# A spectral filter beside a gated MLP on one core: a stored order of instructions, four-tile butterflies, and final sums copied by ScalarE

## The chip, the cores and the metric

The kernel runs on one NeuronCore of a Trainium2 chip. The core has five engines with a queue of their own each: TensorE (PE, matmul), VectorE (DVE), ScalarE (ACT), GpSimd (POOL) and SyncE (SP), which here issues the DMAs. An engine takes its instructions in the order in which they stand in its queue, and waits on semaphores for what others produce. The metric is device time in microseconds of one execution; lower is better.

## The reference

For x of 2048 rows and 640 columns (bf16) two branches are computed on the normalised rows and added to x:

```python
xn = _layernorm(x, axis=-1)
return x + _A_ref(xn, A_w_r, A_w_i) + _B_ref(xn, B_w_gate, B_w_up, B_w_down)
# A: X = rfft2(xn) * (w_r + 1j*w_i); irfft2(X) to bf16
# B: g = xn @ w_gate; u = xn @ w_up; (g * u) @ w_down      640 -> 1536 -> 640
```

A is a two-dimensional Fourier transform over rows and columns, a product with a spectrum of weights, and the way back. B is a gated MLP without an activation function.

## The kernel before

The 2048 rows lie in 16 row tiles of 128 partitions. Everything is held on chip; only inputs, tables and outputs cross to HBM.

Start. The rows are loaded (`_X_LOADS`), normalised by tile (L767 and L776 on ScalarE, or L785 and L794 on VectorE, for the statistics; L807, L811, L817 for the inverse deviation; L824 subtracts, L831 scales), and transposed: the first four tiles on TensorE (L849), the other twelve by DMA (L837). While nothing is ready, TensorE runs 40 matmuls on zeros (L749) and, behind the first transpose, 44 small filler matmuls (L738). The gate and up projections of the first four tiles use 128 or 256 columns at a time (L998), the rest 512 columns (L978). Their results are copied from PSUM by a helper (L718 where ScalarE does it, L719 where VectorE does) and multiplied on VectorE (L1014, L1015).

Row transform. A column transform of 640 points is split into butterflies on VectorE and matmuls. The forward butterflies work on two row tiles at a time: five tasks S1 to S5, 14 instructions (L891 to L925), eight groups. R (L938) is the matmul that follows, for each row tile.

Middle. Only when all 16 tiles have passed R may D begin (L1056), then C (L1079), the product with the spectrum of weights WM on VectorE (L1094, L1097), a negation NG (L1106, L1107) and reversed copies NS on GpSimd (L1114 to L1116), then IA, the inverse (L1130, L1131). This runs over 16 steps t of two q each. The spectrum is loaded in a ring of three buffers.

End. I (L1159) for each row tile, then the inverse butterflies V1 to V5, two row tiles at a time (L1183 to L1216, 13 instructions, eight groups), whose last result is the branch's bf16 value. For each row tile and half of its columns, ACC (L1237) sums twelve down-projection matmuls in one PSUM bank, and IV (L1249) adds the spectral branch with one more matmul. FIN (L1257) adds x from PSUM on VectorE, half by half, and SP stores each half.

What sets the order. The kernel is written as tasks with engine choices, durations, priorities and reads and writes. `plan` (L155) is a list scheduler that runs while the kernel is built: it picks one task after another by priority and earliest start, chooses the engine and the PSUM bank (with a cap on banks per class, such as two for L998's and three for the middle's tasks), and drops fillers that no longer fit. `compute_waits` (L339) then puts in the semaphore waits. What is built is a fixed order on each engine; L1272 calls the scheduler. The order decides all below.

```python
sch.caps = {"glu": opts.get("cap_glu", 4), "acc": opts.get("cap_acc", 5), "fill": 1}
...
sch.plan(8, filler_deadline=opts.get("fill_deadline", 7600.0))
sch.compute_waits()
```

Of the kernel before, what the change touches and what calls it, by code (L numbers as in the profile page):

```python
# [17 lines left out]
_DMA_ISSUE = 500.0  # L18


class _Task(object):
    __slots__ = ("tid", "name", "engs", "dur", "emit", "prio", "deps", "nleft", "succ", "bank", "frees",
                 "freers", "eng", "start", "end", "seq", "units", "nbytes", "semkey", "semval", "cls", "vc",
                 "waits")
# [47 lines left out]
class _Sched(object):  # L72
    def __init__(self):
        self.tasks = []
        self.bufs = []
        self.caps = {}
        self.window = 250.0
        self.affinity = 600.0
        self.dma_bw = _DMA_BW
        self.slack = {"pe": 1000.0, "act": 300.0, "dve": 400.0, "pool": 100.0, "sp": 0.0}  # L80
        self.order = None
        self.urgent = ()
        self.makespan = 0.0
# [71 lines left out]
    def plan(self, nbanks=8, filler_deadline=0.0):  # L155
        tasks = self.tasks
        for t in tasks:
            t.succ = []
        for t in tasks:
            t.deps.discard(t)  # L160
            for d in t.deps:
                d.succ.append(t)
            t.nleft = len(t.deps)
        eng_free = dict((e, _START) for e in _ENGS)
        seq = dict((e, 0) for e in _ENGS)
        banks = [[0.0, None] for _ in range(nbanks)]
        held_by_cls = {}
        avail = [t for t in tasks if t.nleft == 0]
        pending_free = {}
        for t in tasks:  # L170
            if t.bank is not None:
                if not t.freers:
                    raise RuntimeError("task %s takes banks but nothing frees them" % t.name)
                pending_free[t.tid] = len(t.freers)
        free_end = {}
        dma_pipe = 0.0
        order = dict((e, []) for e in _ENGS)
        nsch = 0
        ntot = len(tasks)
        dropped = []  # L180

        def choose(kind):
            best = None
            if kind == "pair":
                for k in range(0, nbanks, 2):
                    a_, b_ = banks[k], banks[k + 1]
                    if a_[0] is None or b_[0] is None:
                        continue
                    ft_ = max(a_[0], b_[0])
                    if best is None or ft_ < best[0]:  # L190
                        best = (ft_, k)
            else:
                for k in range(nbanks):
                    st = banks[k]
                    if st[0] is None:
                        continue
                    partner = banks[k ^ 1]
                    pen = 0.0 if partner[0] is None else 1.0
                    key = (pen, st[0])
                    if best is None or key < best[2]:  # L200
                        best = (st[0], k, key)
            return best

        def release(p):
            k0 = p.units[1]
            nb = 2 if p.units[0] == "pair" else 1
            for k in range(k0, k0 + nb):
                banks[k][0] = free_end[p.tid]
                banks[k][1] = list(p.freers)
            held_by_cls[p.cls] -= 1  # L210

        while nsch < ntot:
            cands = []
            for t in avail:
                unit_choice = None
                bank_ready = 0.0
                if t.bank is not None:
                    cap = self.caps.get(t.cls)
                    if cap is not None and held_by_cls.get(t.cls, 0) >= cap:
                        continue  # L220
                    ch = choose(t.bank)
                    if ch is None:
                        continue
                    unit_choice = (t.bank, ch[1])
                    bank_ready = ch[0]
                    if bank_ready > 0.0:
                        bank_ready += _XLAT["pe"]
                best = None
                for ei, e in enumerate(t.engs):
                    est = eng_free[e]  # L230
                    for d in t.deps:
                        lat = _SLAT[e] if d.eng == e and not d.nbytes else _XLAT[e]
                        if d.eng == e and e == "pe":
                            lat = -_TAIL[e]
                        de = d.end + lat
                        if de > est:
                            est = de
                    if bank_ready > est:
                        est = bank_ready
                    fin = est + t.dur[e]  # L240
                    score = fin + (self.affinity if ei > 0 else 0.0)
                    if best is None or score < best[3]:
                        best = (est, fin, e, score)
                cands.append((best[0], best[1], best[2], t, unit_choice))
            real = [c for c in cands if c[3].cls != "fill"]
            if not cands or (not real and nsch + len([a_ for a_ in avail if a_.cls == "fill"]) < ntot
                             and not any(c[3].cls == "fill" for c in cands)):
                raise RuntimeError("scheduler deadlock: %d/%d scheduled, avail=%s" % (
                    nsch, ntot, [a_.name for a_ in avail][:10]))
            pick = None  # L250
            by_eng = {}
            for c in cands:
                by_eng.setdefault(c[2], []).append(c)
            for e_ in by_eng:
                lst = by_eng[e_]
                hb = None
                for c in lst:
                    k = (c[3].prio, c[0], c[3].tid)
                    if hb is None or k < hb[0]:
                        hb = (k, c)  # L260
                hc = hb[1]
                slack = self.slack.get(e_, 100.0)
                if hc[3].name in self.urgent:
                    slack = 100.0
                ch_ = None
                for c in lst:
                    if c is hc or c[1] <= hc[0] + slack:
                        k = (c[0], c[3].prio, c[3].tid)
                        if ch_ is None or k < ch_[0]:
                            ch_ = (k, c)  # L270
                c = ch_[1]
                k = (c[0], c[3].prio, c[3].tid)
                if pick is None or k < pick[0]:
                    pick = (k, c)
            est, fin, e, t, unit_choice = pick[1]
            if t.cls == "fill" and (est > filler_deadline or not real):
                for f in [a_ for a_ in avail if a_.cls == "fill"]:
                    avail.remove(f)
                    dropped.append(f)
                    nsch += 1  # L280
                    for s_ in f.succ:
                        s_.deps.discard(f)
                        s_.nleft -= 1
                        if s_.nleft == 0:
                            avail.append(s_)
                continue
            t.eng = e
            t.start = est
            if t.nbytes:
                issue_end = est + t.dur[e]  # L290
                ds = max(issue_end + _DMA_LEAD, dma_pipe)
                de = ds + t.nbytes / self.dma_bw
                dma_pipe = de
                t.end = de + _DMA_LAT
                eng_free[e] = issue_end
            else:
                t.end = fin + _TAIL[e]
                eng_free[e] = fin
                seq[e] += 1
            t.seq = seq[e]  # L300
            order[e].append(t)
            if unit_choice is not None:
                k0 = unit_choice[1]
                nb = 2 if unit_choice[0] == "pair" else 1
                for k in range(k0, k0 + nb):
                    st = banks[k]
                    if st[1] is not None:
                        for fr in st[1]:
                            t.deps.add(fr)
                    st[0] = None  # L310
                t.units = unit_choice
                held_by_cls[t.cls] = held_by_cls.get(t.cls, 0) + 1
            if t.bank is not None and t in t.freers:
                pending_free[t.tid] -= 1
                fe = free_end.get(t.tid, 0.0)
                if t.end > fe:
                    free_end[t.tid] = t.end
                if pending_free[t.tid] == 0:
                    release(t)
            for p in t.frees:  # L320
                pending_free[p.tid] -= 1
                fe = free_end.get(p.tid, 0.0)
                if t.end > fe:
                    free_end[p.tid] = t.end
# [8 lines left out]
        for f in dropped:  # L333
            self.tasks.remove(f)
# [48 lines left out]
_D = 640  # L383
# [966 lines left out]
```

## Time and profile before

| what | value |
|---|---|
| median of 3 runs | 204.6 us (204.39 to 204.77) |
| span of the profiled execution | 202.8 us (its own total is not listed; the median is 1.8 above) |
| instructions | 4769 |
| first transpose on TensorE (L849) | 5.55 us |
| first 512-column projection (L978) | 22.94 us |
| first matmul of the middle (L1056) | 82.44 us |
| last matmul (L1249) starts | 200.26 us |
| bytes moved by DMA | 23.82 MB |
| granted TensorE clock | 1.00 throughout |

A line of the page or of the timeline names the engine, the source line, the operation, the tile written and read (here nearly all are views of one big buffer, `arena`, or of PSUM, `ps`), the shape, and the count. Times are microseconds from the start of the span. In the table of waits, "A <- B: total, times, longest" says that A's engine stood idle until B ended. A matmul's duration holds its latency, so a row of matmuls is better read by the distance of their starts.

### The profile page before, as it was taken

Reading aid. Unit: us, or ns where it says so; the run is one execution under the profiler, and the core shown is the slowest. Engines: PE = TensorE matmul, PEld = TensorE weight load, DVE = VectorE, ACT = ScalarE, POOL = GpSimd, SP = SyncE. Lnnn points to the kernel's source line nnn. Section 1 sums busy time; section 2 is a strip of 40 time slices with the busy share of each in tenths; the row PEclk is TensorE's granted clock in tenths of the full one; section 3 lists DMA queues with packets and bytes.
Section 4 is the critical chain, followed back from the end, with each engine's and each line's share of the span. In section 5 each row is a group of like instructions: output and inputs, shape, how many; then the busy total and the mean of one; then the engine's idle time right before and its main releaser. Section 6 shows DMA issues by size and latency. Waiting matters only on the chain.

```text
span 202.8 us, 4769 instructions
## 1 busy us (share of the span) xinstructions
PE 198.0 (98%) x1785; PEld 128.1 (63%) x1785; DVE 179.5 (89%) x511; ACT 127.5 (63%) x277; POOL 32.0 (16%) x108
## 2 busy tenths in 40 slices
PE   7999999999999999899999999999999999999995
PEld 7987644454444555556666666667777767777774
DVE  3599999999999997697988898864999999999983
ACT  3678899999975776869999999987611220200000
POOL 0000000000000000075754675453000000000000
DMA  6999983031161597605354444004313332332222
GB/s 183 300 341 378 377 80 65 3 65 32 32 63 39 112 276 194 197 14 132 74 145 114 103 102 127 0 5 136 92 32 97 106 107 66 113 90 81 93 65 65
DMA packets 31542, 23.82 MB, mean 117 GB/s; under 512 B 10528, under 2 KB 29472, under 8 KB 31392
## 3 DMA queue, kind: packets, MB, share of 16 engines
q1 hardware_dynamic: 30720, 23.16, 43.5%
q10 hardware_dynamic: 800, 0.36, 0.6%
q8 instruction: 14, 0.23, 0.5%
q14 instruction: 8, 0.07, 0.1%
HBM read 18.92 MB, written 2.62 MB: 106 GB/s over the span
## 4 chain that ended last, share of the span: by engine, by line
PE 85%; DVE 5%; SPq 4%; DMA 4%; issue 1%; ACT 1%
PE ps L978 44%; PE ps L1237 23%; SPq L712 4%; DMA arena<-in_A_x_dram 4%; PE ps L1131 3%; PE ps L1130 3%; PE ps L998 2%; PE ps L1079 2%; PE ps L938 2%; PE ps L1159 2%; PE ps L1249 2%; PE ps L1056 2%; DVE arena L719 1%; DVE arena L1257 1%; DVE arena L1186 0%
## 5 line engine op out<-in xcount | busy, mean ns | idle before, releaser
L718 ACT ACTIVATE arena<-ps 128x512 bf16<-128x512 f32 (+7 forms) x206 | 104.8, 547 | 40.1 <-PE ps L1159 24.0
L978 PE MATMUL ps<-arena 128*128 128x512 bf16 x420 | 97.0, 379 | 0.1
L978 PEld LDWEIGHTS ps<-arena 128*128 128x128 bf16 x420 | 38.9, 98 | 41.9 <-ACT arena L718 1.4
L1237 PE MATMUL ps<-arena 128*128 128x320 bf16 (+2 forms) x396 | 56.5, 295 | 0.2 <-DVE arena L1257 0.2
L1237 PEld LDWEIGHTS ps<-arena 128*128 128x128 bf16 x396 | 37.6, 98 | 13.9 <-DVE arena L1257 0.5
L1094 DVE TENSOR_TENSOR arena<-ps,arena 128x256 bf16<-128x256 f32 x64 | 24.0, 416 | 0.1
L1014 DVE TENSOR_TENSOR arena<-arena 128x512 bf16<-128x512 bf16 x42 | 17.7, 421 | 4.7 <-ACT arena L718 4.7
L1107 POOL TENSOR_SCALAR arena<-arena 128x256 bf16<-128x256 bf16 x8 | 6.8, 855 | 89.3 <-DVE arena L1097 89.2
L719 DVE CAST arena<-ps 64x321 bf16<-64x321 f32 (+1 forms) x25 | 12.2, 490 | 6.3 <-PE ps L1131 5.8
L1257 DVE TENSOR_TENSOR arena<-ps,arena 128x320 bf16<-128x320 f32 (+2 forms) x33 | 15.4, 473 | 1.8 <-PE ps L1249 1.8
L998 PE MATMUL ps<-arena 128*128 128x128 bf16 (+1 forms) x160 | 14.4, 246 | 0.4 <-ACT arena L718 0.4
L1130 PEld LDWEIGHTS ps<-arena 128*128 128x128 bf16 x160 | 12.4, 114 | 2.8 <-ACT arena L718 0.4
L998 PEld LDWEIGHTS ps<-arena 128*128 128x128 bf16 x160 | 12.0, 98 | 2.1 <-ACT arena L718 1.2
L1130 PE MATMUL ps<-arena 128*128 128x64 bf16 x160 | 13.3, 196 | 0.0
L1131 PE MATMUL ps<-arena 128*128 128x64 bf16 x160 | 13.3, 197 | 0.0
L1131 PEld LDWEIGHTS ps<-arena 128*128 128x128 bf16 x160 | 11.2, 113 | 2.1
L1116 POOL TENSOR_SCALAR arena<-arena 128x65 bf16<-128x65 bf16 x32 | 12.1, 378 | 0.0
L1114 POOL COPY arena<-arena 128x63 bf16<-128x63 bf16 x32 | 8.6, 268 | 17.1 <-DVE arena L1097 17.0
L1097 DVE TENSOR_TENSOR arena<-ps,arena 128x130 bf16<-128x130 f32 x32 | 9.3, 292 | 0.0
L776 ACT ACTIVATE arena<-arena 128x640 bf16<-128x640 bf16 x11 | 9.1, 824 | 0.0
L1115 POOL COPY arena<-arena 128x63 bf16<-128x63 bf16 x32 | 9.0, 280 | 0.0
L891 DVE TENSOR_TENSOR arena<-arena 128x384 f32<-128x384 bf16 x16 | 8.8, 552 | 0.0
(62 smaller groups left out, 221.0 us busy)
## 6 DMA issues: line engine op xcount, KB each, us to landing
arena<-in_A_x_dram SPq DMA_DIRECT2D x20, 160.0 KB, 2.4
out_dram<-arena SPq DMA_DIRECT2D x31, 80.0 KB, 1.6
arena<-in_A_w_r_dram SPq DMA_DIRECT2D x8, 160.5 KB, 3.0
arena<-in_A_w_i_dram SPq DMA_DIRECT2D x8, 160.5 KB, 3.0
arena<-in_B_w_gate_dram SPq DMA_DIRECT2D x4, 320.0 KB, 5.8
arena<-in_A_x_dram SPq DMA_DIRECT2D x1, 1280.0 KB, 9.8
arena<-in_A_w_r_dram SPq DMA_DIRECT2D x14, 80.2 KB, 2.9
arena<-in_A_w_i_dram SPq DMA_DIRECT2D x14, 80.2 KB, 3.1
```

The lines of the kernel that those rows point to most:

```text
L718: return c.e.activation(dst, src, _ACTF.Copy)
L719: return c.e.tensor_copy(dst, src)
L978: ins = c.e.matmul(ps[:, bk, :], v_gw[:, w, j, ft, :], v_xt[:, j, rows], start=(j == 0), stop=(j == 4))
L998: ins = c.e.matmul(ps[:, bk, w * n:(w + 1) * n], v_gw[:, w, j, ft, :], v_xt[:, j, rows], start=(j == 0), stop=(j == 4))
L1014: return c.e.tensor_tensor(v_ht[:, ft0, rows], v_gbf[:, rr, 0, :], v_gbf[:, rr, 1, :], _OP.mult)
L1094: c.e.tensor_tensor(dst, xh.unsqueeze(1).to_broadcast([128, 2, 32, 4]), wv, _OP.mult)
L1097: return c.e.tensor_tensor(d5, x5, wg[:, :, 0:321:5], _OP.mult)
L1116: return c.e.tensor_scalar(yg[:, 128:193], yg[:, 256:321], -1.0, None, _OP.mult)
L1130: c.e.matmul(dst, l1, v_ti[:, q, 0, :], start=True, stop=False)
L1131: ins = c.e.matmul(dst, l2, v_ti[:, q, 1, :], start=False, stop=True)
L1237: ins = c.e.matmul(ps[:, bk, 0:sl3.stop - sl3.start], v_ht[:, ft, a * 128:(a + 1) * 128], v_wd[:, ft, sl3], start=(ft == _FT_ORDER[0]), st ...
L1257: return c.e.tensor_tensor(v_out[:, a % 2, sl3], ps[:, bk, 0:sl3.stop - sl3.start], v_xr[:, xs, sl3], _OP.add)
```

## The change

Four things are done together.

1. `plan` is removed, and with it the caps, the slack and the priorities' effect. `replay` takes a table `_PLAN` of (task, engine, bank) triples, written into the file by an offline search, and lays the tasks out in that order. Waits are computed as before.
2. The forward and inverse butterflies work on groups of up to four row tiles (`_S_GROUPS`, `_V_GROUPS`): 2, 2, 4, 4, 4 forward and 4, 4, 4, 2, 2 inverse. Temporaries are no longer double, except the inverse input; one addition of V2 moves into V4, which writes in place.
3. For row tiles 0 to 14 the finished sum is copied from PSUM by ScalarE, half by half, into the output buffer; VectorE then adds x to the whole tile, and one DMA stores it. Tile 15 stays as it was, in three pieces.
4. Smaller ones: the layer norm's statistics are fp32; epsilon is the bias of Sqrt, set once on GpSimd; from tile 4 on, subtraction and scaling are one instruction; tile 1's statistics move from ScalarE to VectorE; 36 warm-up matmuls for 40, and 12 filler matmuls (three tasks of four) for 44; the first up-weights are issued by SP, not ScalarE. The durations that the tasks carry are changed too; with a stored order they affect only which semaphore waits are left out as implied.

```diff
-_DMA_ISSUE = 500.0
+_DMA_ISSUE = 540.0
...
-    def plan(self, nbanks=8, filler_deadline=0.0):
...
+    def replay(self, plan):
+        by = dict((t.tid, t) for t in self.tasks)
...
+        for tid, ei, bk in plan:
+            t = by.pop(tid)
+            t.deps.discard(t)
+            e = _ENGS[ei]
...
+                for k in range(bk, bk + (2 if t.bank == "pair" else 1)):
+                    if owner[k] is not None:
+                        t.deps |= set(owner[k].freers)
+                    owner[k] = t
+                t.units = (t.bank, bk)
...
+_S_GROUPS = ((0, 2), (2, 2), (4, 4), (8, 4), (12, 4))
+_V_GROUPS = ((0, 4), (4, 4), (8, 4), (12, 2), (14, 2))
...
+_PLAN = (
+    (14, 4, -1), (8, 2, -1), (21, 2, -1), (0, 1, -1), (177, 4, -1), (9, 3, -1), (15, 4, -1), (20, 2, -1), (22, 2, -1),
...
+                if va:
+                    return c.e.activation(v_sd[:, sl_], v_ss[:, sl_], _ACTF.Sqrt, bias=v_eps, scale=1.0 / _D)
+                return c.e.activation(v_sd[:, sl_], v_mv[:, sl_, 1], _ACTF.Sqrt, bias=v_eps)
...
+                    return c.e.tensor_scalar(v_x[:, b, :], v_x[:, b, :], mean, v_rs[:, b:b + 1], _OP.subtract, _OP.mult)
...
-                    q="act" if w_ and i < 1 else "sp")
+                    q="act" if w_ and i < opts.get("gw_act", 0) else "sp")
...
+            def em_v2(c, gr=gr, nt=nt, n=n):
+                a_ = v_tc[:, gr, 4, 0:nt].rearrange("p u n -> p (u n)")
+                return c.e.scalar_tensor_tensor(v_vy[:, 0:n], v_vt[:, 0, 0:n], -0.25, a_, _OP.mult, _OP.add)
...
+            def em_v4(c, gr=gr, nt=nt, n=n):
+                ej = v_tc[:, gr, :, 0:nt].rearrange("p s u n -> p s (u n)")
+                a_ = ej[:, 4]
+                c.e.tensor_tensor(a_, v_vt[:, 0, 0:n], a_, _OP.add)
+                c.e.tensor_tensor(ej[:, 3:1:-1], v_vq[:, :, 0:n], v_vt[:, 2:4, 0:n], _OP.add)
+                return c.e.tensor_tensor(ej[:, 0:2], v_vq[:, :, 0:n], v_vt[:, 2:4, 0:n], _OP.subtract)
...
+                def em_f0(c, own=own, a=a, sl3=sl3):
+                    return copy_on(c, v_out[:, a % 2, sl3], ps[:, bank_of(own), 0:sl3.stop - sl3.start])
+                T("FINA_%d_%d" % (a, hf), "act", _d_act(c1 - c0), em_f0, writes=[(b_out, rb[0])],
...
+                def em_f2(c, a=a, xs=xs):
+                    return c.e.tensor_tensor(v_out[:, a % 2], v_out[:, a % 2], v_xr[:, xs, :], _OP.add)
...
+        sch.replay(_PLAN)
```

## The prediction

> **What bounds the kernel now.** I read the busy table first, then the chain of waits in order of time, then the timeline of the start, and then the windows of the three long stages with the table of waits.
>
> ```profile
> PE 198.0 (98%) x1785; PEld 128.1 (63%) x1785; DVE 179.5 (89%) x511; ACT 127.5 (63%) x277; POOL 32.0 (16%) x108
> PE 85%; DVE 5%; SPq 4%; DMA 4%; issue 1%; ACT 1%
> ```
> ```profile
> 41.49 0.56 PE ps L938 x10
> 42.05 7.55 PE ps L978 x35
> ...
> 193.39 4.48 PE ps L1237 x33
> ```
>
> TensorE owns the chain and streams without gaps inside a group: 7.55/35 = 0.216 us per 512-column matmul, 0.56/10 = 0.056 per 128, 4.48/33 = 0.136 per 320. "98% busy" hides gaps, because each matmul counts its latency too. So I price the stream itself. From the same chain: 0.031 per 64 columns, 0.137 per 321; 0.109 for 256 lies between the 128 and 512 rows. The necessary matmuls, by stage:
>
> - start: 20 transposes, 80x128, 80x256 columns: 14.3 us
> - gate/up with row transform (255 L978, 80 L938): 59.7
> - middle (165 L978, 160 L1056, 32 L1079, 320 L1130/L1131, 5 L1237): 55.4
> - end (391 L1237, 80 L1159, 33 L1249): 60.35
>
> Together 189.7 us, which the change does not alter. The first transpose starts at 5.55, L978 at 22.94, L1056 at 82.44, the last of the middle ends at 139.34, the last matmul's stream at 200.3. So the time lost is 22.94 - 5.55 - 14.3 = 3.05; 0 (-0.15 by rounding); 139.34 - 82.44 - 55.4 = 1.5; 200.3 - 139.34 - 60.35 = 0.6. About 5.0 us in all, plus 5.55 before and 202.8 - 200.3 = 2.5 after. More than that 5.0 the change cannot win except at the two rims.
>
> ```profile
> 6.03 1.84 PE L738 MATMUL ps<-arena 128*128 128x64 bf16 x44
> 6.28 0.36 DVE L719 COPY arena<-ps 128x384 bf16<-128x384 bf16 x1 [0.88 <-PE ps L849]
> 6.57 0.36 ACT L718 ACTIVATE arena<-ps 128x256 bf16<-128x256 bf16 x1
> 7.71 1.28 PE L998 MATMUL ps<-arena 128*128 128x128 bf16 x20
> ...
> 18.25 4.86 PE L998 MATMUL ps<-arena 128*128 128x256 bf16 x40 [0.40 <-ACT arena L718]
> ```
>
> Both copies of the first transposed tile have ended by 6.93, but TensorE is still in 44 filler matmuls and starts the projection at 7.71.
>
> ```profile
> 30.00:80.00 50.00, 50.00 (x281) 24.20 (x280) 49.67 (x147) 40.91 (x86) 0.00 (x0) 1.00 0.40 82
> 84.00:138.00 54.00, 53.31 (x625) 32.67 (x624) 46.31 (x143) 49.70 (x116) 31.21 (x102) 1.00 0.33 85
> 142.00:198.00 56.00, 55.82 (x448) 40.81 (x446) 54.93 (x132) 8.51 (x13) 0.00 (x0) 1.00 0.29 85
> ```
> ```profile
> DVE arena L719 <- PE ps L1131: 5.8, 7, 1.0
> ```
>
> Columns: length, then busy PE, weight load, DVE, ACT, POOL. VectorE is full beside a full TensorE in the first and third window, while ScalarE idles in the third; in the middle ScalarE is full, and VectorE waits for the inverse transform once in each round.
>
> **What the Trainium skill says.** "TensorE: Matmul & The Clock Gate", Back-to-back issue gap: N/2.4 + 2.5 ns warm; the 0.216 and 0.136 us above agree. Same page, Part 1 (the HAM clock gate): about 3.4 us of activity release the full clock; here matmuls step at 0.107 us to 5.9 and at 0.056 from 7.71, so cutting warm-up work is a risk. "VectorE: DVE Perf Modes", The perf-mode tier table: a bf16 tensor_tensor runs 2x from SBUF, 1x with a PSUM operand; the trace agrees (L1014, 512 columns, 421 ns; L1257, 320 columns from PSUM, 483 ns). "Perfetto Trace Analysis", Tensor Engine Instruction: ScalarE and VectorE are strict FIFO, so a late item in the new fixed order holds all behind it; the L719 waits above are that.
>
> **The change part by part.** VectorE prices are start to start, about 0.08 us under the mean durations: 256 fp32 columns 0.34 (L909 at 20.47, L910 at 20.81), 512 0.61, so about 0.07 fixed per instruction plus 1.05 ns a column.
>
> Butterflies over four tiles: 8 groups of 14 forward and 13 inverse instructions (216) become 5 groups (135). The columns stay; 81 x 0.07 = 5.7 us of VectorE saved. Cost: later first results and one set of temporaries. The first inverse chain takes 13 instructions: 8 x 0.61 + 2 x 1.13 + 1.40 + 0.87 + 0.61 = 10.0 us, plus one H (0.34), a copy of 0.75 and crossings, 11.4. In the changed kernel's built order, 15 L978, 58 L1237 and 20 L1159 (numbers of the kernel before, here and below) lie between the fourth tile's L1159 and the first L1249: 3.2 + 7.9 + 1.1 = 12.2 us, so the chain hides with 0.8 to spare; uncovered, each us costs one.
>
> Final sums: 31 x 0.41 us on VectorE become 30 ScalarE copies of 0.33 (the pitch of L718 at 320 columns) and 15 bf16 adds of 640 columns, 0.41 by L1014's 0.34 for 512. VectorE gains about 6 us, ScalarE takes 10 where its window shows 8.5 busy of 56. The new chain copy, add, 160 KB store (landing 2.4 us as for L712's 160 KB) before the buffer returns is about 6 us per two tiles against 7 us of TensorE; hidden on average. The last tile keeps the old path: the 2.5 us tail stays.
>
> Layer norm: subtract and scale fused for 12 tiles (12 x 0.31), epsilon as Sqrt's bias, no variance helper: 5 us less VectorE. If the fused form lost its fast mode it would cost 0.73 instead of 0.31, 5 us back; I take 0.31 since both single forms have it with pointer scalars.
>
> Against these, VectorE takes over PSUM copies: 14 of 512 columns (0.62), 6 of 640 (0.75), 4 of 320 (0.46), less 10 of 321 (0.45), some 10 us. Its total falls only by 5.7 + 6 + 5 - 10, from about 177 to 171. What decides is each stage:
>
> Start: 12 fillers instead of 44, the first tile's ScalarE copy no longer behind tile 1's statistics, up-weights moved from ScalarE's queue to fourth on SP's. Bytes ahead of those weights are unchanged, about 1.0 MB, moved by 5.4 at the trace's rate; landing trails such counts by 1 us (tile 2's 1.82 MB at 8.05, VectorE released at 9.11). So the first projection can go at 6.8 (bound: 6.7 by the copies, 7.7 if the weights were as late as the fillers). The next weights bind then, 8.3 to 9.1, against 9.11 now. The later losses (1.0 us, mostly ScalarE holding PSUM banks while it does statistics) should halve with free bank choice. The loss of 3.05 becomes 1.75 (1.2 to 3.0).
>
> Gate/up with row transform: 215 L978 stand before the first L1056, 51.0 us. VectorE must end its last forward group: from 17.0 (tile 4's load landed at 16.88) 51.6 us of work, 68.6, with TensorE at that point at 70.6: hidden by 2 us. SP is nearer. From the last normalised tile (57.0 by the same sum) it issues 5 transposes (1.2 each, L837) and 13 spectrum-weight loads (0.63 each, from 2.58 for 4), the last from 70.6 to 71.2, landing 2.9 to 5.2 later for such loads: 73.5 to 76.4, where TensorE wants the first L1079 at 74.7. I charge 0.3 (0 to 1.7).
>
> Middle: 155 L978 and the same rest, 52.5 us. VectorE from first L1056 copy to last L1094 group: 64 x 0.34 + 32 x 0.21 + 14 H x 0.34 + 10 x 0.18 + 9 copies of 512 at 0.62 + 9 x 0.46 + 8 x 0.45 = 48.4; with 0.35 before and 1.5 after, 2.3 us of waiting are free. Now: 46.5 of work in 54.7, so 8.2 us of waiting. ScalarE by the same sum falls from full to about 45 of 52.5 and answers sooner. I take 3.3 us of waits, so 1.0 lost (0 to 6.0).
>
> End: 50 L978 move here, 71.85 us, with 53 us of VectorE: no longer tight. Loss 0.5 (0.2 to 1.5) for banks.
>
> Sum: 5.5 + 189.7 + 1.75 + 0.3 + 1.0 + 0.5 + 2.5 = 201.2 us of span, 1.6 under 202.8. The page gives no total for the profiled execution; the runs' median, 204.6, is 1.8 above its span. I carry 1.8 over: 203.0.
>
> **The rivals.** (a) The order closes nearly all gaps: start 1.2, then 0, 0.3, 0.2: 199.4 + 1.8 = 201.2. For it: TensorE has filler of its own in every stage, and no cap on banks per class binds. Against: in-order queues lose something in each round now.
>
> (b) SP is late: the first L1079 waits the full 1.7, in place of 0.3, with another 0.2 behind it: 204.6, no change. For it: the sum above leaves nothing. Against: landing is 2.9 at most sizes.
>
> (c) Slower: VectorE becomes the bound in the middle. If it waits for TensorE's results as long as now (8.2 us), the stage takes 0.35 + 48.4 + 8.2 + 1.5 = 58.5, 6.0 above its matmuls, 5.0 more than I charge: 208.0. It decides from 4.9 us of waits (a stage loss of 2.6). For it: strict FIFO and 92% of work in the window. Against: ScalarE, which fed those waits, is lighter.
>
> **How the numbers follow.** Forecast 203.0 (202.2 to 204.1): 0.44. (a) 0.20, (b) 0.15, (c) 0.21. Two tenths of a per cent, about what a measurement can tell, is 0.4 us. Faster: nearly all of the forecast, (a), some of (b): 0.66; same, mostly (b): 0.13; slower: (c): 0.21. The range runs from somewhat under (a), 200.6, into the lower part of (c), 206.2.
>
> **What would show it.** First projection near 6.8 and L978's successor near 21.6; first L1056 near 72.9; VectorE's waits in the middle near 3 us, and ScalarE below 90%; VectorE with visible idle after 140. Wrong if TensorE steps at 0.107 after 7 us, if the fused normalisation shows over 0.5 us, or if L1079's successor waits for a DMA.

## The result, and the profile after

The changed kernel takes 207.69 us (205.65 to 208.25, 4 runs) against 204.62 of the kernel before on the same chip: a ratio of 1.013 (1.008 to 1.018). Measured again later beside 41 runs of the kernel before, it gave 208.41 (206.26 to 210.54, 6 runs), ratio 1.0133 (1.0092 to 1.0175). Medians and ranges here and below take in every run; the ratios leave out the few that took over 1.5% more than the fastest of their kernel. The forecast was 203.0, its range 200.6 to 206.2: wrong by 4.7 us, and wrong in sign.

The busy table and the chain of waits of the changed kernel, with the row of granted clock (40 slices of 5.15 us, in tenths):

```profile
PE 197.4 (96%) x1749; PEld 128.0 (62%) x1749; DVE 175.9 (85%) x400; ACT 127.4 (62%) x283; POOL 34.8 (17%) x113
PEclk9999999999999999999999699999999999999999
PE 86%; DMA 6%; DVE 4%; SPq 1%; issue 1%
```

TensorE is busy for 96% where it was 98%, DMA has 6% of the chain where it had 4%, and one slice, around 116 us, has a clock of 0.6. The lines have new numbers: L818 is L849 of the kernel before (the transpose), L968 is L998 and L948 is L978 (the projections), L1026 is L1056 (D), L1049 is L1079 (C), L1064 and L1067 are the product WM, L1101 is the inverse, L1206 the down-projection, L1218 the matmul that adds the spectral branch, L679 issues the loads, and L685 and L686 are the copies on ScalarE and VectorE. Cut into the prediction's stages by the starts of the timeline (first L818 at 5.43, first L948 at 22.25, first L1026 at 73.40, end of the middle's last L1101 stream at 131.88, stream of the last matmul, L1218, ended by 203.68):

| part | before | forecast | after |
|---|---|---|---|
| before the first transpose | 5.55 | 5.5 | 5.43 |
| loss in the start | 3.05 | 1.75 | 22.25 - 5.43 - 14.3 = 2.5 |
| loss in gate/up with row transform | 0 | 0.3 | 73.40 - 22.25 - 51.0 = 0.15 |
| loss in the middle | 1.5 | 1.0 | 131.88 - 73.40 - 52.5 = 6.0 |
| loss in the end | 0.6 | 0.5 | 203.68 - 131.88 - 71.85 = -0.05, that is 0 |
| tail | 2.5 | 2.5 | 2.4 |

One term is far off: the middle. The windows of the three long stages (length, then busy PE, weight load, DVE, ACT, POOL, clock, DMA share, GB/s) and VectorE's waits in the middle:

```profile
22.20:73.40 51.20, 51.20 (x298) 25.48 (x297) 50.65 (x101) 44.22 (x96) 0.00 (x0) 1.00 0.36 84
75.00:132.00 57.00, 53.81 (x645) 33.34 (x643) 48.26 (x147) 45.88 (x106) 34.50 (x108) 0.97 0.48 113
135.00:203.00 68.00, 68.00 (x520) 47.71 (x518) 55.90 (x94) 21.68 (x46) 0.00 (x0) 1.00 0.26 79
```
```profile
DVE arena L686 <- PE ps L948: 3.5, 2, 3.0
DVE arena L1064 <- PE ps L1049: 2.8, 4, 1.1
DVE arena L686 <- PE ps L1101: 2.0, 2, 1.2
```

VectorE waits 8.3 us in the middle. That is what rival (c) assumed (8.2), and its time, 208.0, is the measured one. But VectorE waits for TensorE here, so the next question is what TensorE waits for. Its timeline around 112 us:

```profile
107.21 0.31 PE L1049 MATMUL ps<-arena 128*128 128x321 bf16 x1 [0.59 <-DMA arena<-in_A_w_i_dram]
...
111.67 0.31 PE L1026 MATMUL ps<-arena 128*128 128x64 bf16 x5
113.90 0.30 PE L1049 MATMUL ps<-arena 128*128 128x321 bf16 x1 [1.91 <-DMA arena<-in_A_w_i_dram]
...
114.17 2.01 PE L948 MATMUL ps<-arena 128*128 128x512 bf16 x5
```

L1049 is C, the matmul whose result is multiplied with the spectrum. C does not read the spectrum itself, but the kernel's `hold` lets it start only when what its product reads is there, so a late load stops TensorE. C waits 0.59 and 1.91 us for spectrum loads, and the first C waits 0.69 at 75.4 us: 3.2 in all. (The view calls the last one "issue"; the last load of that group goes out at 73.5 and lands at 76.0, and C starts at 76.07.) Behind the gap of 1.91 us five L948 take 1.80 us to the next L1049 at 115.97, in place of 1.08. Windows of half a microsecond (length, busy PE, clock, DMA share, GB/s) show why:

```profile
113.00:113.50 0.50, 0.00 (x0) 1.00 1.08 190
...
114.00:114.50 0.50, 0.50 (x8) 1.00 1.07 218
114.50:115.00 0.50, 0.50 (x3) 0.51 0.85 160
...
117.50:118.00 0.50, 0.50 (x3) 0.57 0.00 0
```

From 114.5 to 117.9 the granted clock is half: 3.4 us at 0.5 cost 1.7. So 3.2 + 1.7 = 4.9 of the 6.0 lost are late transfers and the lowered clock behind one of them. Now the queue that issues it, SyncE's:

```profile
98.45 1.24 SPq L679 DMA_DIRECT2D arena<-in_A_w_i_dram  x2
99.73 1.25 SPq L679 DMA_DIRECT2D arena<-in_A_w_r_dram  x2
101.02 0.60 SPq L679 DMA_DIRECT2D arena<-in_A_w_i_dram  x1
101.66 1.18 SPq L679 DMA_DIRECT2D arena<-c_ti  x1
103.30 0.60 SPq L679 DMA_DIRECT2D arena<-in_A_w_i_dram  x1
103.96 1.24 SPq L679 DMA_DIRECT2D arena<-in_A_w_r_dram  x2
105.23 0.59 SPq L679 DMA_DIRECT2D arena<-in_B_w_down_dram  x1
106.13 0.59 SPq L679 DMA_DIRECT2D arena<-in_A_w_r_dram  x1
106.77 1.90 SPq L679 DMA_DIRECT2D arena<-in_A_w_i_dram  x3
```

These lines must be read beside the table. The spectrum comes in groups of six loads, one group for two steps t, into a ring of three buffers. I call the groups by the step they begin with: w0 (eight loads), w2, and so on to w14. A group's first load makes SyncE wait until VectorE has used up what lay in the buffer. The kernel before issues each group together, as here:

```profile
97.88 1.83 SPq L712 DMA_DIRECT2D arena<-in_A_w_r_dram  x3
99.76 1.89 SPq L712 DMA_DIRECT2D arena<-in_A_w_i_dram  x3
```

The table does this (SyncE's entries alone, from the first load that waits):

```
w6 w6 w6 | w8 | w6 w6 w6 | w10 | w8 w8 | w10 | w8 w8 | w10 | w8 | w12 | w10 | w12 | w10 | w12 | c_ti |
w10 | w12 w12 | w_down (800 KB) | w14 | w12 | w14 w14 w14 w14 w14
```

The load issued first at 106.77 is w12's last. Its buffer had been free since w12's first load went out at 98.45, but ahead of it in the queue stand c_ti (512 KB), w_down (800 KB, first needed near 134) and w14's first, which waits for VectorE until 106.13 (that wait itself lasts 0.3 us here). It lands 7.0 us after its issue, at 113.8, and the C at 113.90 waits for the whole group. The C at 107.21 waits for w10's last load, issued at 103.30 behind w12's first and c_ti in the same way.

### The profile page after: what moved, and what is told of

Same layout as the page of the kernel before. It is cut to its first block, busy times and chain, and to the rows that moved or that the text cites. A ratio compares the mean times of both kernels' runs of the same rounds, so it can differ in the third digit from the quotient of the medians.

```text
span 206.1 us, 4569 instructions
## 1 busy us (share of the span) xinstructions
PE 197.4 (96%) x1749; PEld 128.0 (62%) x1749; DVE 175.9 (85%) x400; ACT 127.4 (62%) x283; POOL 34.8 (17%) x113
## 4 chain that ended last, share of the span: by engine, by line
PE 86%; DMA 6%; DVE 4%; SPq 1%; issue 1%
PE ps L948 40%; PE ps L1206 25%; PE ps L968 6%; DMA arena<-in_A_w_i_dram 3%; DMA arena<-in_B_w_up_dram 3%; PE ps L908 2%; PE ps L1129 2%; PE ps L1218 2%; PE ps L1049 2%; PE ps L1101 2%; PE ps L1100 2%; PE ps L1026 2%; DVE arena L1064 2%; DVE arena L686 1%; SPq L679 1%
## 5 line engine op out<-in xcount | busy, mean ns | idle before, releaser
L685 ACT ACTIVATE arena<-ps 128x512 bf16<-128x512 f32 (+6 forms) x222 | 108.0, 528 | 68.2 <-PE ps L1218 35.1
L948 PE MATMUL ps<-arena 128*128 128x512 bf16 x420 | 99.6, 383 | 0.0
L948 PEld LDWEIGHTS ps<-arena 128*128 128x128 bf16 x420 | 39.5, 98 | 40.2 <-issue 1.2
L1206 PE MATMUL ps<-arena 128*128 128x320 bf16 (+2 forms) x396 | 57.8, 295 | 0.0
L1206 PEld LDWEIGHTS ps<-arena 128*128 128x128 bf16 x396 | 37.8, 98 | 14.4
L1064 DVE TENSOR_TENSOR arena<-ps,arena 128x256 bf16<-128x256 f32 x64 | 24.0, 415 | 3.0 <-PE ps L1049 2.8
L686 DVE CAST arena<-ps 128x512 bf16<-128x512 f32 (+3 forms) x34 | 19.5, 578 | 6.0 <-PE ps L948 3.5
L1084 POOL COPY arena<-arena 128x63 bf16<-128x63 bf16 x32 | 8.4, 263 | 90.5 <-DVE arena L1067 90.5
L968 PE MATMUL ps<-arena 128*128 128x128 bf16 (+1 forms) x160 | 13.8, 246 | 1.8 <-DVE arena L782 1.2
L1245 DVE TENSOR_TENSOR arena<-arena 128x640 bf16<-128x640 bf16 x15 | 7.1, 487 | 8.3 <-ACT arena L685 8.3
L968 PEld LDWEIGHTS ps<-arena 128*128 128x128 bf16 x160 | 12.2, 98 | 2.9 <-issue 2.1
L1101 PE MATMUL ps<-arena 128*128 128x64 bf16 x160 | 13.8, 198 | 0.0
L1100 PEld LDWEIGHTS ps<-arena 128*128 128x128 bf16 x160 | 12.4, 115 | 1.6 <-issue 0.3
L1049 PE MATMUL ps<-arena 128*128 128x321 bf16 x32 | 9.5, 307 | 3.2 <-DMA arena<-in_A_w_i_dram 2.5
L1101 PEld LDWEIGHTS ps<-arena 128*128 128x128 bf16 x160 | 11.6, 114 | 1.1
L1077 POOL TENSOR_SCALAR arena<-arena 128x256 bf16<-128x256 bf16 x12 | 10.2, 854 | 5.0 <-DVE arena L1067 5.0
L1026 PEld LDWEIGHTS ps<-arena 128*128 128x128 bf16 x160 | 7.7, 98 | 3.6 <-issue 0.3
L686 DVE COPY arena<-ps 128x640 f32<-128x640 f32 (+1 forms) x8 | 5.5, 702 | 5.0 <-PE ps L1129 3.7
L1067 DVE TENSOR_TENSOR arena<-ps,arena 128x130 bf16<-128x130 f32 x32 | 9.3, 292 | 0.0
```

The costliest lines, as they stand in the source:

```text
L685: return c.e.activation(dst, src, _ACTF.Copy)
L686: return c.e.tensor_copy(dst, src)
L948: ins = c.e.matmul(ps[:, bk, :], v_gw[:, w, j, ft, :], v_xt[:, j, rows], start=(j == 0), stop=(j == 4))
L968: ins = c.e.matmul(ps[:, bk, w * n:(w + 1) * n], v_gw[:, w, j, ft, :], v_xt[:, j, rows], start=(j == 0), stop=(j == 4))
L1026: ins = c.e.matmul(ps[:, bk, k * 64:k * 64 + n], v_uq[:, k, t, :], v_fd[:, k * 128 + w * n: k * 128 + w * n + n], start=True, stop=True)
L1049: return c.e.matmul(ps[:, bank_of(c.t), 0:_LP], v_tf[:, q, :], v_a[:, ar, 324 * g:324 * g + _LP], start=True, stop=True)
```

## The experiments

All kernels but ops_only keep the changed kernel's order on TensorE, VectorE, ScalarE and GpSimd; those with a filled start run more filler matmuls in it, and grouped_act has one load more on ScalarE's queue. The theories: T1, the order of transfers on SyncE's queue costs the middle its 5 us, by the two large transfers among the spectrum loads; T5, the later form, by loads that stand behind one whose buffer is not free; T2, small loads land late in any order; T3, VectorE and ScalarE bound the middle, as rival (c) had it; T4, the new operations themselves cost; TS, the thinned start lowers the clock. Medians are in microseconds; the ratio is to the kernel before on the same chip.

| label | median (range, runs) | ratio (interval) |
|---|---|---|
| after_again | 208.41 (206.26 to 210.54, 6) | 1.0133 (1.0092 to 1.0175) |
| wd_behind | 205.32 (203.92 to 206.67, 14) | 1.0025 (1.0004 to 1.0047) |
| ti_early | 204.93 (203.22 to 206.23, 14) | 1.0008 (0.9982 to 1.0034) |
| ring_first | 205.52 (204.93 to 210.13, 10) | 1.0049 (1.0030 to 1.0067) |
| order_all | 203.83 (202.90 to 207.89, 13) | 0.9956 (0.9942 to 0.9971) |
| fill_back | 205.71 (204.44 to 210.54, 22) | 1.0045 (1.0029 to 1.0062) |
| order_fill | 203.98 (202.88 to 205.07, 21) | 0.9966 (0.9951 to 0.9981) |
| ops_only | 212.53 (212.30 to 212.80, 4) | 1.0382 (1.0363 to 1.0401) |
| grouped | 203.66 (202.60 to 204.66, 10) | 0.9949 (0.9931 to 0.9967) |
| grouped_all | 202.72 (202.42 to 202.94, 4) | 0.9901 (0.9886 to 0.9916) |
| grouped_act | 202.40 (202.18 to 202.59, 4) | 0.9885 (0.9868 to 0.9901) |
| held_one | 203.48 (202.62 to 204.19, 6) | 0.9934 (0.9913 to 0.9955) |

### One transfer moved at a time

wd_behind moves w_down (task 745) behind w14's loads (707 to 712); 672 is w12's last load. In these diffs only SyncE's entries are listed.

```diff
-    (745, 4, -1), (708, 4, -1), (672, 4, -1), (710, 4, -1), (712, 4, -1), (709, 4, -1), (711, 4, -1), (707, 4, -1),
+    (708, 4, -1), (672, 4, -1), (710, 4, -1), (712, 4, -1), (709, 4, -1), (711, 4, -1), (707, 4, -1), (745, 4, -1),
```

> The changed kernel with one line of its table moved: the 800 KB of w_down, which SyncE issues at 105.2 us directly ahead of the last eight spectrum loads (106.1 to 110.6), is issued behind them. Theory T1 (the middle is lost to the order of the transfers on SyncE's queue: the C matmul at 112.0 waits 1.9 us for a load that lands 7.0 us after its issue): that wait falls under 0.8 us, TensorE's clock is not lowered behind it (0.63 and 0.52 of full speed in 114 to 118 us now), and the time falls by 1.2 to 3.5 us, to 204.2 to 206.5. Rival T2 (the loads land late because of their own small packets, whatever is ahead of them): the wait stays over 1.5 us and the time within 0.5 us of 207.7. Rival T3 (VectorE and ScalarE bound the middle): the wait for the transfer goes but a wait for VectorE or ScalarE of about its length takes its place, time within 0.5 us of 207.7.

ti_early moves c_ti's second half (438) behind w6's last load (556):

```diff
-    (556, 4, -1), (633, 4, -1),
+    (556, 4, -1), (438, 4, -1), (633, 4, -1),
...
-    (674, 4, -1), (438, 4, -1), (635, 4, -1),
+    (674, 4, -1), (635, 4, -1),
```

> The changed kernel with one line of its table moved: the second half of c_ti (512 KB), issued at 101.7 us among the spectrum loads, is issued at about 82.5 us, where SyncE's queue then idles until 86.7. T1: the loads behind it are issued some 1.2 us earlier and see less traffic, the waits of the C matmuls at 107.2 (0.6 us) and 112.0 (1.9 us) fall together by 0.5 to 1.5 us and the time by as much, to 206.2 to 207.2. T2 and T3: within 0.4 us of 207.7.

ring_first puts w0's eight loads ahead of w2's five in the first round, the transposes between them keeping their places:

```diff
-    (442, 4, -1), (481, 4, -1), (439, 4, -1), (483, 4, -1), (444, 4, -1), (479, 4, -1), (443, 4, -1),
-    (446, 4, -1), (484, 4, -1), (445, 4, -1), (480, 4, -1), (441, 4, -1), (440, 4, -1),
+    (439, 4, -1), (440, 4, -1), (441, 4, -1), (442, 4, -1), (443, 4, -1), (444, 4, -1), (445, 4, -1),
+    (446, 4, -1), (481, 4, -1), (483, 4, -1), (479, 4, -1), (484, 4, -1), (480, 4, -1),
```

> The changed kernel with the thirteen first spectrum loads permuted within their own slots on SyncE's queue: the eight that the first C matmul waits for come first, the five of the next ring slot after them. T1: the first C no longer waits at 75.4 (0.7 us now), and the time falls by 0.4 to 0.8 us, to 206.9 to 207.3. T3 (another engine bounds what follows): the wait goes, the time stays within 0.3 us of 207.7.

order_all does all three and moves 672 ahead of 708. (Its expectation gives 672 to the C at 107.2; it is the one at 113.9 that waits for it.)

```diff
-    (708, 4, -1), (672, 4, -1),
+    (672, 4, -1), (708, 4, -1),
```

> The three moves together, and one more: the last load of the sixth ring slot, which the C matmul at 107.2 waits for, is issued ahead of the one that makes SyncE wait until 106.1. All operations, engines and PSUM banks are as in the changed kernel, only the order of transfers on SyncE's queue differs. T1: waits of 0.7, 0.6 and 1.9 us go and with them the lowered clock (about 1.7 us in the profiled run), so the time falls by 3 to 5 us, to 202.7 to 204.7, at or under the kernel before. T3: no more than 1.5 us of it comes back as time, 206 or more; VectorE or ScalarE is then what C and the tasks behind it wait for.

Each single move gave 2.2 to 2.8 us against 207.69, T1 being right on the sign of all of them. These gains are not each move's own, though: fill_back, below, moves no transfer and gains 2.0. T2 and T3 are out. In wd_behind 672 is issued at 107.85, later than in the table, but lands 2.9 us after its issue in place of 7.0, and the wait at 113.90 is gone: what had held this load up most was w_down's bytes in front of it, not its place in the queue. On the sizes T1 was right for w_down and order_all; c_ti and the first ring gave two to three times what it said. c_ti was issued at 89.4, not 82.5: in the table 556 itself stands behind w8's first load. The effects do not add, and the traces show one reason. In ring_first the first C starts at 74.98 without a wait, but another one waits 0.99 at 100.19, and the C at 112.44 then only 0.74: TensorE held up once is late for the next transfer and waits less. And with the wait at 112 shorter, the lowered clock behind it is gone from the profiled run. order_all leaves 0.4 us of waits before C in its profiled run.

### The changed kernel again, the start, and the operations alone

> The changed kernel itself, in five rounds beside the others, to have its time with as many runs as the moves have (four runs gave 207.69, from 205.65 to 208.25). T1, by which the three moves of transfers give 3.9 us together: 207 to 208.3. A rival, T4: the four runs were unlucky and the changed kernel scatters as its variants do (ti_early 203.22 to 206.23), so that it is at 205.5 to 206.5 and the moves give 2 us.

T1 held nearly (208.41, just over its 208.3), and its rival is out. fill_back gives the start its filler matmuls back:

```diff
-                for i in range(4):
-                    ins = c.e.matmul(ps[:, bk, 64 * i:64 * i + 64], v_dum[:, 0:128], v_dum[:, 128:192], start=True,
+                for i in range(12):
+                    ins = c.e.matmul(ps[:, bk, 64 * (i % 4):64 * (i % 4) + 64], v_dum[:, 0:128], v_dum[:, 128:192], start=True,
...
-        nwarm = opts.get("nwarm", 9)
+        nwarm = opts.get("nwarm", 10)
```

> The changed kernel with its start filled as before: ten warm matmul groups in place of nine, and the three fill tasks issue twelve 64-column matmuls each in place of four (36 in all; before had 44, the changed kernel 12). They feed nothing. Theory TS (the clock of 0.992 in some runs is a lowered TensorE clock at 7 to 10.7 us, after 5 to 7.5 us in which TensorE is busy for less than half of the time; the kernel before showed 1.0 in all 39 runs): clock 1.0 at the start in all runs, the time down by 0.2 to 0.8 us. Rival: the fills stand ahead of the first projection and cost what they take where the operands are there earlier: up by 0.1 to 0.5 us.

order_fill is the same edit in order_all.

> order_all with the same filled start. TS: 0.2 to 0.8 us under order_all's 203.83, that is 203.0 to 203.6, with clock 1.0 in all or nearly all runs and less scatter. Rival: no better than 203.8.

The windows of order_all's start (length, busy PE, clock, ...) show what the filler prevents:

```profile
6.50:7.00 0.50, 0.00 (x0) 1.00 0.94 285
7.00:7.50 0.50, 0.00 (x0) 0.69 1.16 350
7.50:8.00 0.50, 0.31 (x4) 0.50 1.12 367
...
10.50:11.00 0.50, 0.50 (x11) 0.89 1.19 299
```

The first projection, at 7.69, runs at half speed until 10.6. The mean clock of a run was 0.992 or below in 4 of 13 runs of order_all and 4 of 10 of grouped, both without the filler; with it, in none of the 35 runs of order_fill, grouped_all, grouped_act and held_one, so on the clock TS held in these. In fill_back, which has the filler as well, it was 0.992 or below in 3 of 22 runs; its profiled run shows 1.00 at the start, and where the clock fell in those three is not known. (The column does not show the very first microseconds: in the kernel before, the 64-column filler steps at 0.053 us until 6.8 and at 0.029 from 6.9 on, both at a clock of 1.00.) Within grouped the runs with a lowered clock take 204.1 in the mean, the others 203.4. On the time TS missed: order_fill scatters less than order_all but is no faster (the intervals of the ratios overlap), while fill_back, with the table's transfers, gained 2.0 us at the median where 0.2 to 0.8 were expected. Why a fuller start shortens the middle (56.6 us from the first L1026 to the first L1129, for 59.6 in the changed kernel's profiled run) is not settled. Under the same order of transfers its C waits 0.40, 0.92 and 0.28 us, 1.6 in place of 3.2, and the clock stays at 1.00 behind them. What the table's order costs thus depends on the start.

ops_only removes the table and puts back the scheduler of the kernel before with its caps, settings and fillers, under the changed kernel's operations:

```diff
-        sch.replay(_PLAN)
+        sch.window = 100.0
+        sch.slack["act"] = opts.get("slack_act", 700.0)
...
+        sch.plan(8, filler_deadline=opts.get("fill_deadline", 7600.0))
```

> The changed kernel's operations (butterflies over four row tiles, fused normalisation, ScalarE's copies of the final sums), but ordered by the list planner of the kernel before with its settings, with its 70 fill tasks and ten warm groups, instead of the table. T1 (the order costs, not the operations): 203.5 to 205.5, no slower than the kernel before by more than 0.5 us. Rival T4 (the operations themselves cost: four-tile butterflies make what follows wait for larger groups): 206 or more, with waits for VectorE in the middle or at the end of over 2 us.

By its numbers T4 won, 212.53. But the waits are others than T4 named: among ScalarE's and TensorE's, in the table of waits,

```profile
ACT arena L759 <- DMA out_dram<-arena: 8.8, 4, 4.1
PEld ps L1022 <- ACT arena L759: 5.7, 16, 0.6
PE ps L1174 <- ACT arena L759: 2.0, 2, 1.4
```

ScalarE's copies (L759 in this kernel) wait in the scheduler's order for an output buffer that is still being stored, and TensorE waits for ScalarE's copies. The scheduler's settings were made for other operations. The run shows that these operations under that scheduler are slower; it does not show that they are slow, and grouped_all shows that they need not be.

### Groups of loads together

grouped permutes the 50 spectrum loads within their own slots, so that each group stands together; c_ti and w_down stay where they are. The part behind w4, with w6 being 555 to 560, w8 593 to 598, w10 631 to 636 and w12 669 to 674:

```diff
-    (555, 4, -1), (560, 4, -1), (557, 4, -1), (593, 4, -1), (558, 4, -1), (559, 4, -1), (556, 4, -1), (633, 4, -1),
-    (598, 4, -1), (597, 4, -1), (636, 4, -1), (596, 4, -1), (594, 4, -1), (632, 4, -1), (595, 4, -1), (673, 4, -1),
-    (634, 4, -1), (670, 4, -1), (631, 4, -1), (674, 4, -1), (438, 4, -1), (635, 4, -1), (669, 4, -1), (671, 4, -1),
-    (745, 4, -1), (708, 4, -1), (672, 4, -1),
+    (555, 4, -1), (560, 4, -1), (557, 4, -1), (558, 4, -1), (559, 4, -1), (556, 4, -1), (593, 4, -1), (598, 4, -1),
+    (597, 4, -1), (596, 4, -1), (594, 4, -1), (595, 4, -1), (633, 4, -1), (636, 4, -1), (632, 4, -1), (634, 4, -1),
+    (631, 4, -1), (635, 4, -1), (673, 4, -1), (670, 4, -1), (438, 4, -1), (674, 4, -1), (669, 4, -1), (671, 4, -1),
+    (745, 4, -1), (672, 4, -1), (708, 4, -1),
```

> The changed kernel with its 50 spectrum loads permuted within their own slots of SyncE's queue so that the loads of one ring slot stand together (in the table one load of the next slot, which makes SyncE wait for VectorE, stands ahead of the last loads of the present slot in every round: at 86.7, 92.7, 98.5 and 106.1 us). c_ti and w_down stay where the table has them. T5 (the queue is in order, so a load whose buffer is free is held behind one whose buffer is not, and the slot is complete only after the next slot's release): the waits before C's matmuls fall from 7.7 us to under 3.5, the clock is lowered in fewer runs, and the time is 204.3 to 206, 2 to 4 us under the changed kernel's 207.7 to 208.4. T1 in its first form (it is the large c_ti and w_down among the loads): most of the waits stay, 206.5 or more.

grouped_all then puts 438 behind 556 and 745 behind 707, and has fill_back's edit.

> Grouped loads, with c_ti's second half early and w_down behind the last spectrum load as in order_all, and the filled start as in order_fill. T5: the two waits of together 2.3 us before C at 96 to 104 us that order_fill still showed go too, and the time is 202.2 to 203.6, below order_fill's 203.98 by 0.4 to 1.8. Rival: what is left in order_fill is VectorE's and ScalarE's, so that another wait takes their place: 203.7 to 204.2.

T5 held, and the time of grouped fell below what it said (203.66 for 204.3 to 206): with the large transfers left in place, grouping alone takes 4.0 us off 207.69, and no wait before C is left. (The 7.7 and 2.3 us of waits in the two expectations add those of C's weight loads to those of its matmuls, 3.2 and 0.9.) But order_all, which moves the large transfers and leaves most loads interleaved, came as far, to 203.83. Either remedy alone comes this far, and the shares of the gates, that is of loads waiting for a buffer, and of the large transfers are not separated. grouped_all takes 5.0 off, with the filled start, and scatters by 0.5 us; against fill_back, which has that start too, its order of transfers is worth 3.0. Its SyncE queue, around the same place:

```profile
97.59 0.61 SPq L679 DMA_DIRECT2D arena<-in_A_w_i_dram  x1
...
101.22 0.60 SPq L679 DMA_DIRECT2D arena<-in_A_w_i_dram  x1
105.27 0.59 SPq L679 DMA_DIRECT2D arena<-in_A_w_r_dram  x1
```

w12 is complete on the queue at 101.22, before SyncE waits for w14's buffer until 105.27. The C rows of both kernels (busy, mean ns, then the idle time before them), the changed kernel first:

```profile
L1049 PE MATMUL ps<-arena 128*128 128x321 bf16 x32 | 9.5, 307 | 3.2 <-DMA arena<-in_A_w_i_dram 2.5 <-issue 0.7
```
```profile
L1049 PE MATMUL ps<-arena 128*128 128x321 bf16 x32 | 9.3, 302 | 0.0
```

VectorE and ScalarE in the middle of grouped_all, and VectorE's waits there:

```profile
75.00:127.00 52.00, 51.96 (x645) 32.95 (x644) 48.28 (x148) 45.83 (x107) 34.37 (x108) 1.00 0.47 123
```
```profile
DVE arena L686 <- PE ps L1101: 2.0, 2, 1.2
DVE arena L1064 <- PE ps L1049: 0.6, 2, 0.4
DVE arena L686 <- PE ps L948: 0.5, 1, 0.5
```

The same VectorE work, 48.3 us, now has 3.1 us of waits in place of 8.3. T3, and with it rival (c), is out: the 5 us of VectorE's waits that went were TensorE's.

grouped_act issues the first half of w_up from ScalarE's queue, as before:

```diff
-    (178, 4, -1),
+    (178, 1, -1),
...
-                    q="act" if w_ and i < opts.get("gw_act", 0) else "sp")
+                    q="act" if w_ and i < opts.get("gw_act", 1) else "sp")
```

> grouped_all with the first half of w_up issued on ScalarE's queue at the start, as in the kernel before, in place of the fourth place on SyncE's. If the start's loss (2.7 us where 1.75 was forecast) is the late issue of that transfer: 0.3 to 0.9 us under grouped_all. If it is the bytes ahead of it (some 300 GB/s moved in 3 to 7 us in either kernel): within 0.3 us of grouped_all.

It is 0.32 us below grouped_all, and the intervals overlap, so it lies on the border between the two expectations. The first L948 starts at 21.9 for 22.2. The first half of w_up lands at 6.2 in place of 7.2, but tile 1's rows at 6.6 in place of 5.0, and the first projection goes at 7.86 for 7.29: what one load gains, the next ones lose. The Trainium skill, "DMA: Bandwidth & Descriptors", Issuing engines are not separate DMA queues, says that issuing from several engines saves only the time to initiate; the trace agrees, with issues of about 0.5 us here and a gain in time that is not clear of noise.

held_one puts the table's habit back into grouped_all, for one load a group. In the first of the four rounds the held load, 556, comes to stand behind the second half of c_ti (438) as well:

```diff
-    (556, 4, -1), (438, 4, -1), (593, 4, -1),
+    (593, 4, -1), (438, 4, -1), (556, 4, -1),
...
-    (595, 4, -1), (633, 4, -1),
+    (633, 4, -1), (595, 4, -1),
...
-    (635, 4, -1), (673, 4, -1),
+    (673, 4, -1), (635, 4, -1),
...
-    (672, 4, -1), (708, 4, -1),
+    (708, 4, -1), (672, 4, -1),
```

> grouped_all with one thing of the table put back: in four rounds the last load of a ring slot is issued behind the first of the next slot, whose buffer is not free yet. T5: each such load then lands 3 to 5 us later, the C matmuls of the slots concerned wait 0.3 to 1 us each where they come close behind, and the time is 0.5 to 2.5 us over grouped_all. Rival: one load held back is hidden, within 0.3 us of grouped_all.

It costs 0.8 us at the median, though the two intervals just touch and the profiled run is the slowest of the six. C has one wait in the middle, where grouped_all has none:

```profile
93.55 0.31 PE L1049 MATMUL ps<-arena 128*128 128x321 bf16 x1 [1.02 <-DMA arena<-in_A_w_r_dram]
```

This C waits for 556, which goes out at 87.4 (83.2 in grouped_all), behind 593's wait for its buffer and behind c_ti, and lands at 93.5, 6.1 us later (2.8 in grouped_all). The other three held loads, which land 3 to 6 us later than in grouped_all, cost TensorE no wait. So the 1.0 us is a gate and a large transfer together, not the gate alone. Four loads held back cost 0.8; the table's whole habit with its two large transfers costs 3.0 with the same filled start, and 4 to 5 without it. Traffic is part of that: a 160 KB load of w_i took 7.0 us to land in the changed kernel from 105 to 107.3 us, and 3.4 in grouped_all from 98 to 116.

## Why the prediction was wrong

**Where it failed.** "Middle: ... I take 3.3 us of waits, so 1.0 lost (0 to 6.0)." The stage was priced by VectorE's work and waits alone. Its transfers were not walked through. I had counted SyncE's queue for the first ring ("5 transposes ... and 13 spectrum-weight loads"), where it cost 0.69 us, but not for the six rounds behind it, in which the order of entries, readable in the table before any run, puts loads behind another buffer's release and behind 1.3 MB of c_ti and w_down. In the profiled run this took the loss from 1.0 to 6.0: 3.2 us of waits before C, 1.7 of lowered clock, and 1.1 that neither explains. With the same loads grouped and nothing else changed (grouped), the middle loses 127.71 - 74.40 - 52.5 = 0.8. The 6.0 is not the order's alone, since with a filled start the table's order loses about 3 (fill_back); how the start reaches into the middle stays open.

**The rest of the sum stood.** In grouped_all the middle loses 126.68 - 73.34 - 52.5 = 0.84 us (forecast 1.0), VectorE waits 3.1 (3.3), ScalarE is 88% busy (below 90%), and the kernel takes 202.72 (203.0). With the loads grouped and the start filled, then, the changed kernel is about 1.9 us faster than the kernel before, as forecast. That the sum agrees within 0.3 is in part luck: the start loses 0.8 more than its term, and gate/up, the middle and the end together 0.9 less. How much of the 1.9 is order and how much operations was not separated.

**Start.** Mis-sized: 1.75 against 2.5, and 2.5 again in grouped_all. The first projection went at 7.38 (forecast 6.8). The view puts its wait of 1.16 us down to a reciprocal on VectorE, but the first half of w_up, issued at 2.20, lands 5.1 us later, at 7.3, where the prediction had its bytes moved by 5.4 and landed 1 us after that. The next group at 9.61 waited 0.68 for w_up's second half. The risk named ("cutting warm-up work") came true in some runs, at about 7 to 11 us.

**Gate/up, end.** 0.15 and 0.0 lost against 0.3 and 0.5. The fused normalisation has a median of 437 ns, below the 0.5 us that would have shown it slow. VectorE's busy time fell by 3.6 us, from 179.5 to 175.9, where some 6 were forecast; in the window of the end it is busy for 55.9 of 68 us, idle as forecast.

**The rivals.** (b) had the right engine and place for its first wait, SyncE at the first C, and only 0.69 of the time. (c) hit the time, 208.0, and VectorE's 8.2 us of waits, by luck: the runs exclude its mechanism. The prediction's own test, "if L1079's successor waits for a DMA", is what decided.

## What to carry to other kernels

Where a stored or searched order interleaves transfers on one queue, list for every load the latest gate (wait for a buffer) that stands ahead of it, not its own, and the bytes issued shortly before it: a group is complete only after the last gate ahead of its last member, and lands late behind a large transfer. Keep the loads of one buffer together, and large transfers that are needed much later behind them or in the queue's idle time. An engine that waits as long as a theory says is no proof of it; follow the wait to whoever is not waiting for anyone.

## What the runs showed of the hardware

A gap of TensorE need not be long to cost its clock. In the changed kernel's profiled run TensorE is idle for 1.9 us from 112.0, and half clock follows from 114.5, when it is busy again, for 3.4 us. The Trainium skill, "TensorE: Matmul & The Clock Gate", HAM oscillation — how this bites in real kernels, gives as the rule no idle gaps over some 3.4 us; this gap was shorter, so the measurement decides. The gap of 1.16 us at 6.2 in the same run had no such effect. At the start, half clock lasted 3.4 us as well in the profiled runs of order_all (7.2 to 10.6), wd_behind (7.5 to 10.9) and grouped (7.8 to 11.2).

Of the changed kernel's ten runs, four had a mean clock of 0.999 or 1.0 (206.5 us in the mean), four 0.992 (208.3), and two 0.984 (209.4 and 210.5). The step of about 1.7 us from the first four to the next fits one such stretch each, 3.4 us at half speed; which gap caused it in the runs without a profile is not known.

A load of 160 KB lands 2.9 us after its issue or 7.0, depending on what was issued just before it: the same load, 672, in wd_behind and in the changed kernel, where 800 KB of w_down went out 1.5 us ahead of it.
